# Zero products and a new order in the first pairs' chains, and the first two tiles' activations kept by slots

## The chip, the cores and the metric

The kernel runs on one core of a Trainium2 chip. The core has a matrix engine (TensorE, PE in the profile; PEld is its weight load), three engines that work on elements (VectorE is DVE, ScalarE is ACT, GpSimd is POOL), and a queue engine, SyncE (SP), that here only issues DMA transfers. ACT issues DMA transfers too, between its copies. PE writes to PSUM, eight banks of 2 KB a partition, and DVE or ACT must copy a result out before a bank is used again. The metric is the device time of one execution in microseconds (us). Three timed runs of the kernel before gave 237.89, 238.70 and 238.92 us, a median of 238.7 us.

## The reference

Two layers follow each other. The first is a linear attention with decay (4 batches, 8 heads, 768 positions, head size 64); the second a bilinear feed-forward layer on the 3072 tokens that come out of it.

```python
gamma = 1.0 - 2.0 ** (-5.0 - np.arange(H))
for t in range(S):
    state = gamma[None, :, None, None] * state + np.einsum('bhd,bhe->bhde', k[:, :, t], v[:, :, t])
    y[:, :, t] = scale * np.einsum('bhd,bhde->bhe', q[:, :, t], state)
x = y.transpose(0, 2, 1, 3).reshape(B * S, H * D)        # 3072 x 512
out = (x @ w_a) * (x @ w_b) @ w_out                       # 512 -> 1536 -> 512
```

Inputs and outputs are float32; the kernel multiplies in bfloat16.

## The kernel before

**Attention.** Tokens are cut into 24 slots of 128 positions, six to a batch. Within a slot the recurrence is written as a masked product: scores of k and q, a mask, a product with v (`intra`), and a product of q with the state from earlier slots (`inter`); `update` adds the slot to the state. The decay is put into k and q by tables (`scaled`, L211, k times ktab and q times qtab).

The first six slots, the whole of batch 0, are handled as three pairs (`casts2`, `flip2`, `scores2`, `update2`, `intra2`, `inter2`, `leave2`): one load brings 256 positions with even and odd positions side by side, so that a pair's scores come out by even and odd. `casts2` makes the bfloat16 copies `kqb` (K is index 0, Q is index 1) and `vb`; `flip2` transposes them on PE (L348) and copies the result to `kqT`; `scores2` makes `at` (L361) and masks it on DVE into `aT` (L367); `leave2` copies the result `y` into `xt`, one half on ACT (L177) and one on DVE (L179), and in copying it puts even and odd positions back into natural order.

**Feed-forward.** `TILES = [4, 2, 4, 4, 4, 4, 2]` groups the slots into seven tiles of 512 or 256 tokens. Pairs 0 and 1 are tile 0, pair 2 is tile 1. For a tile and each of 12 blocks `ft` of 128 hidden units, `ffn_a` makes the first product (L429) and ACT copies it to `asb` (L432); `ffn_g` makes the second (L439) and DVE multiplies both into `ht` (L441). `ffn_out` makes 128 tokens of the output (L455), ACT copies them to `osb` (L177) and then issues the store of 256 KB to `out` on its own queue (L461). There are four `osb` buffers.

**Order.** `seq` fixes the program order of every engine as written, so each engine works strictly in that order. Loads are issued on SP in the order of `LOADS`: pairs p0 and p1, weights w0 to w4 (POOL casts them, L179), pair p2, w5, the six parts of `w_out`, then slots s6 to s11. From slot 10 on, SP also transposes `kqb` by DMA (L225), and behind the transpose of slot t it issues the loads of slot t+2 (L91).

The first two pairs and tile 0's first blocks are written out by hand. Pair 2 is worked on after block 9 of tile 0, beside blocks 10 and 11. Then `run` works through lists: tile 1's 12 blocks, the four outputs of tile 0 and the two of tile 1 with the turns of slots 6 to 9 between them, then tile 2. In what follows store 0 to store 5 are these six outputs, in order.

**Waits.** DMA transfers report on eight semaphores. The built program gives each transfer one of the eight, and a transfer that is the next on a semaphore waits, on the engine that issues it, until the earlier transfer on it has landed. Loads on SP and stores on ACT share them. In the built program of before, store 0 waits in this way for the v load of slot 8, store 1 for the v load of slot 9, stores 2, 3 and 4 for an earlier store, and store 5 for the q load of slot 13. PSUM for `a`, `g`, `o`, `tp` and some `at` comes in turn from three banks (`psff`); `y` has two banks and the pairs' first `at` two more.

Of the kernel before, what the change touches and what calls it, by code (L numbers as in the profile page):

```python
# [9 lines left out]
F32 = mybir.dt.float32  # L10
BF16 = mybir.dt.bfloat16
# [13 lines left out]
def kernel(  # L25
# [10 lines left out]
    nc = tc.nc  # L36
    P = 128
    B, H, S, D = q.shape
    NCH = S // P
    HP = H // 2  # L40
    DM = H * D
    DFF = moe_w_a.shape[1]
    KT = DM // P
# [29 lines left out]
    def seq(bi):  # L73
        ins = bi.ins
        prev = last.get(ins.engine)
        if prev is not None:
            tc.add_manual_dep(ins, prev.name, nosync, reason="program order")
        last[ins.engine] = ins
        return bi
# [36 lines left out]
    def issue_loads(n):  # L116
        for _ in range(min(n, len(pending))):
            what = pending.pop(0)
            {"p": load_pair, "s": load_slot, "w": load_w, "o": load_o}[what[0]](int(what[1:]))
# [2 lines left out]
    kqb = {}  # L122
    kqb = {}
    issue_loads(6)
    lgr = const.tile([P, 1, H], F32, name="lgr")
    bq = const.tile([P, 1], F32, name="bq")
    for h in range(H):
# [47 lines left out]
    def cast(engine, dst, src):  # L175
        if engine is nc.scalar:
            seq(nc.scalar.copy(dst, src))  # L177
        else:
            seq(engine.tensor_copy(dst, src))  # L179
# [12 lines left out]
    xt, where = {}, {}  # L192
# [7 lines left out]
    def scaled(eng, t, i):  # L200
        ktab, qtab = tabs[0] if t < 2 * PAIRS else tabs[1]
        dst, src, tab = kqb[t][:, i], raws["kq"[i], t], (ktab, qtab)[i][:, t % NCH]
        if t < 2 * PAIRS:
            dst, src = (x.rearrange("p (hp r) d -> p hp r d", r=2) if x is src else x
                        for x in (dst, src))
            tab = tab.rearrange("p (hp r) o -> p hp r o", r=2).to_broadcast([P, HP, 2, D])
        else:
            dst = dst.rearrange("p hp r d -> p r hp d")
            src = src.rearrange("p (r hp) d -> p r hp d", r=2)
            tab = tab.rearrange("p (r hp) o -> p r hp o", r=2).to_broadcast([P, 2, HP, D])  # L210
        seq(eng.tensor_tensor(dst, src, tab, op=ALU.mult))  # L211
# [121 lines left out]
    def casts2(u, on):  # L333
        for t in (2 * u, 2 * u + 1):
            new_nat(t)
        for (i, par), eng in on.items():
            scaled(eng, 2 * u + par, i)
        for t in (2 * u, 2 * u + 1):
            cast(nc.gpsimd, vb[t], raws["v", t])

    def flip2(u, i, on):
        if i == 0:
            kqT2[u] = tra.tile([P, 2, 2, HP, P], BF16, tag="kqT2", name="kqT2", bufs=2)
        for pars, eng in on:
            tp = psff.tile([P, 2, HP, P], BF16, tag="ff", name="tp")[:, : len(pars)]
            for n, par in enumerate(pars):
                for hp in range(HP):
                    seq(nc.tensor.transpose(tp[:, n, hp, :], kqb[2 * u + par][:, i, hp, :, :], ident))  # L348
            cast(eng, kqT2[u][:, pars[0] : pars[0] + len(pars), i], tp)
# [37 lines left out]
    def inter2(u):  # L387
        for c in range(2):
            if (u, c) == (0, 0):
                continue  # L390
            for hp in range(HP):
                seq(nc.tensor.matmul(ys[u][c][:, hp, :], gbd[c][:, hp, :],
                                     kqT2[u][:, :, 1, hp, half(c)], start=False, stop=False,
                                     skip_group_check=True))

    def intra2(u, par, begin):
        if begin:
            ys[u] = [psat.tile([P, HP, P], F32, tag=f"y{c}", name="y") for c in range(2)]
        t = 2 * u + par
        for hp in range(HP):  # L400
            for r in range(2):
                for c in range(2):
                    seq(nc.tensor.matmul(ys[u][c][half(r), hp, :], vb[t][half(c), 2 * hp + r, :],  # L403
                                         aT[t][half(c), r, hp, :],
                                         start=(begin and hp == 0), stop=not begin,
                                         skip_group_check=True))

    def leave2(u):
        J, i = where[2 * u]
        if i == 0:  # L410
            xt[J] = xtp.tile([P, KT, 4 * P], BF16, tag="xt", name="xt")
        for c, eng in enumerate((nc.scalar, nc.vector)):
            cast(eng,
                 xt[J][:, :, (i + c) * P : (i + c + 1) * P].rearrange(
                     "p k (n two) -> p k two n", two=2),
                 ys[u][c].rearrange("p k (two n) -> p k two n", two=2))

    ht = {}

# [2 lines left out]
    def ffn_a(J, ft, c0=0, c1=None):  # L422
        c1 = TILES[J] * P if c1 is None else c1
        if J not in ht:
            ht[J] = htp.tile([P, NFT, 4 * P], BF16, tag="ht", name="ht")
        fs = slice(ft * P, (ft + 1) * P)
        a = psff.tile([P, 4 * P], F32, tag="ff", name="a")[:, : c1 - c0]
        for kt in range(KT):
            seq(nc.tensor.matmul(a, wa_bf[:, kt, fs], xt[J][:, kt, c0:c1],  # L429
                                 start=(kt == 0), stop=(kt == KT - 1)))  # L430
        asb = asbs[J, ft, c0] = asbp.tile([P, 4 * P], BF16, tag="asb", name="asb")[:, : c1 - c0]
        seq(nc.scalar.copy(asb, a))  # L432

    def ffn_g(J, ft, c0=0, c1=None):
        c1 = TILES[J] * P if c1 is None else c1
        fs = slice(ft * P, (ft + 1) * P)
        g = psff.tile([P, 4 * P], F32, tag="ff", name="g")[:, : c1 - c0]
        for kt in range(KT):
            seq(nc.tensor.matmul(g, wb_bf[:, kt, fs], xt[J][:, kt, c0:c1],  # L439
                                 start=(kt == 0), stop=(kt == KT - 1)))  # L440
        seq(nc.vector.tensor_tensor(ht[J][:, ft, c0:c1], g, asbs.pop((J, ft, c0)), op=ALU.mult))  # L441

# [4 lines left out]
    def ffn_out(J, i):  # L447
        n0 = (sum(TILES[:J]) + i) * P
        osb = osbp.tile([P, DM], F32, tag="osb", name="osb")
        ends = J == len(TILES) - 1 and i == TILES[J] - 1  # L450
        cols = [(0, DM // 2), (DM // 2, 3 * DM // 4), (3 * DM // 4, DM)] if ends else [(0, DM)]
        for c0, c1 in cols:
            o = psff.tile([P, DM], F32, tag="ff", name="o")[:, : c1 - c0]
            for ft in range(NFT):
                seq(nc.tensor.matmul(o, ht[J][:, ft, i * P : (i + 1) * P], wo_bf[:, ft, c0:c1],  # L455
                                     start=(ft == 0), stop=(ft == NFT - 1)))
            cast(nc.vector if c0 == DM // 2 else nc.scalar, osb[:, c0:c1], o)
            if c0 == DM // 2:
                continue
            b0 = DM // 2 if c0 else 0  # L460
            seq((nc.sync if c0 else nc.scalar).dma_start(out=out[n0 : n0 + P, b0:c1],  # L461
                                                         in_=osb[:, b0:c1]))

    def run(work, todo, ahead=4):
        order = []
# [10 lines left out]

    D_, G_, A_ = nc.vector, nc.gpsimd, nc.scalar
    K, Q = 0, 1
    casts2(0, {(K, 1): D_, (K, 0): D_, (Q, 1): D_, (Q, 0): D_})
    flip2(0, K, [((0, 1), A_)])  # L480
    flip2(0, Q, [((1,), D_), ((0,), D_)])
    scores2(0, 1)
    scores2(0, 0, True)
    update2(0, 0)
    casts2(1, {(K, 0): G_, (K, 1): G_, (Q, 0): G_, (Q, 1): D_})
    intra2(0, 1, True)
    inter2(0)
    intra2(0, 0, False)
    leave2(0)
    flip2(1, K, [((0, 1), A_)])  # L490
    update2(0, 1)
    flip2(1, Q, [((1,), D_), ((0,), D_)])
    scores2(1, 0)
    scores2(1, 1, True)
    update2(1, 0)
    cast_w(0)
    W2 = 2 * P
    intra2(1, 0, True)
    inter2(1)
    ffn_a(0, 0, 0, W2)  # L500
    ffn_a(0, 1, 0, W2)
    intra2(1, 1, False)
    leave2(1)
    issue_loads(100)
    cast_w(1)
    ffn_g(0, 0, 0, W2)
# [5 lines left out]
    for ft in range(2, NFT):  # L512
        if ft == 3:
            late_tables()
        if ft % FPW == 0 and ft // FPW + 1 < NW - 1:
            cast_w(ft // FPW + 1)
        if ft == 8:
            casts2(2, {(K, 0): G_, (Q, 0): G_})
            cast_w(NW - 1)
        if ft < 10:  # L520
            ffn_ab(0, ft)
        if ft == 8:
            scaled(D_, 5, K)
            scaled(D_, 5, Q)
    flip2(2, K, [((0, 1), A_)])
    flip2(2, Q, [((0, 1), D_)])
    scores2(2, 0)
    update2(2, 0)
    ffn_a(0, 10)
    scores2(2, 1)  # L530
    ffn_a(0, 11)
    intra2(2, 0, True)
    inter2(2)
    ffn_g(0, 10)
    intra2(2, 1, False)
    leave2(2)
    ffn_g(0, 11)
    for j in range(NO):
        cast_o(j)
# [46 lines left out]
```

## Time and profile before

| | |
|---|---|
| median of three timed runs | 238.7 us (237.89 to 238.92) |
| the profiled execution | 237.4 us, span 235.7 us |
| PE busy | 219.6 us, 93% of the span |
| DVE, ACT, POOL busy | 41%, 35%, 33% |
| DMA moved | 38.59 MB, mean 164 GB/s |
| first product | 6.5 us after the start |
| tile 0's full-width blocks begin | 24.2 us |
| tile 1's first block | 47.0 us |
| tile 2's first block | 78.8 us |

The profile is one execution. A group of instructions has a line, an engine, its tiles, a count and a duration; what stands in brackets is the idle time of the engine before it and what ended that. "ACTq" and "SPq" are transfers being issued on ACT and SP. "DMA share" in the windows is the mean number of packets in flight at one of 16 DMA engines, so it can be over 1. The granted clock of TensorE reads 1.00 in every stretch.

### The profile page before, as it was taken

The numbers are of one execution on the slowest core, as the hardware profiler recorded it, in microseconds if no ns is written. First come the engines' busy times: TensorE is split into PE (matmuls) and PEld (weight loads), VectorE is DVE, ScalarE is ACT, GpSimd is POOL, SyncE is SP. The second block draws the span as 40 slices with busy tenths as digits, with TensorE's granted clock in tenths as the row PEclk, the third lists the DMA queues.
The fourth block names the chain that finished last, engine by engine and source line by source line (L and its number), as shares of the span: only waits on it lengthen the run. The fifth ranks groups of instructions, "written<-read, shape, count | busy, mean of one in ns | idle before, by whom it ended". The sixth has DMA issues, their size and how long they took to land.

```text
span 235.7 us, 4955 instructions
## 1 busy us (share of the span) xinstructions
PE 219.6 (93%) x2021; PEld 121.6 (52%) x2044; DVE 96.1 (41%) x170; ACT 83.2 (35%) x162; POOL 78.6 (33%) x99
## 2 busy tenths in 40 slices
PE   0788997999999899999999999999999999999995
PEld 0566444488555344545454544454544444445874
DVE  3766347655254055634045640155630124310530
ACT  2243523443114423524234521344512242312422
POOL 3385766787763454445335530000000000000000
PEclk9999999999999999999999999999999999999999
DMA  6999999999999999999999982200002200012102
GB/s 179 290 333 352 335 273 376 342 198 219 234 260 211 245 252 172 243 181 257 210 255 172 230 93 89 89 4 0 3 0 89 89 3 0 0 47 89 45 3 89
DMA packets 91894, 38.59 MB, mean 164 GB/s; under 512 B 71776, under 2 KB 87392, under 8 KB 91872
## 3 DMA queue, kind: packets, MB, share of 16 engines
q1 hardware_dynamic: 88416, 32.12, 64.4%
q10 hardware_dynamic: 3456, 6.16, 7.3%
q8 instruction: 16, 0.26, 0.5%
q14 instruction: 6, 0.05, 0.1%
HBM read 28.31 MB, written 6.29 MB: 147 GB/s over the span
## 4 chain that ended last, share of the span: by engine, by line
PE 77%; DMA 11%; DVE 5%; issue 2%; SPq 2%; POOL 1%; ACT 1%; ACTq 0%; DVEq 0%; POOLq 0%
PE g L439 24%; PE a L429 24%; PE o L455 20%; DMA kf<-in_k_dram 6%; DMA qf<-in_q_dram 5%; PE at L254 2%; PE y L299 1%; DVE aT L367 1%; POOL kqb L211 1%; SPq L91 1%; PE tp L348 1%; PE st L270 1%; PE y L403 1%; DVE ht L441 1%; DVE kqT L179 1%
## 5 line engine op out<-in xcount | busy, mean ns | idle before, releaser
L441 DVE TENSOR_TENSOR ht<-g,asb 128x512 bf16<-128x512 f32 (+1 forms) x86 | 52.0, 604 | 109.8 <-PE g L439 88.7
L439 PE MATMUL g<-xt,wb_bf 128*128 128x512 bf16 (+1 forms) x340 | 76.0, 344 | 1.7 <-ACT asb L432 0.8
L429 PE MATMUL a<-xt,wa_bf 128*128 128x512 bf16 (+1 forms) x334 | 75.3, 344 | 0.8 <-DVE xt L179 0.2
L432 ACT CAST asb<-a 128x512 bf16<-128x512 f32 (+1 forms) x86 | 44.2, 517 | 69.4 <-PE a L429 63.6
L455 PE MATMUL o<-wo_bf,ht 128*128 128x512 bf16 (+2 forms) x303 | 63.7, 362 | 0.5
L439 PEld LDWEIGHTS <-wb_bf 128*128 128x128 bf16 x344 | 33.4, 98 | 30.3 <-issue 1.3
L429 PEld LDWEIGHTS <-wa_bf 128*128 128x128 bf16 x344 | 32.7, 98 | 27.9 <-DVE xt L179 0.7
L455 PEld LDWEIGHTS <-ht 128*128 128x128 bf16 x312 | 29.2, 98 | 31.5
L177 ACT COPY osb<-o 128x512 f32<-128x512 f32 (+2 forms) x25 | 14.1, 565 | 53.2 <-PE o L455 41.2
L211 POOL TENSOR_TENSOR kqb<-kf,ktab 128x512 bf16<-128x512 f32 x21 | 21.9, 1044 | 26.6 <-DMA kf<-in_k_dram 26.6
L211 POOL TENSOR_TENSOR kqb<-qf,qtab 128x512 bf16<-128x512 f32 x20 | 21.4, 1068 | 3.1 <-DMA qf<-in_q_dram 2.4
L259 DVE TENSOR_TENSOR aT<-at,mask 128x512 bf16<-128x512 f32 x36 | 22.3, 680 | 0.0
L179 POOL CAST vb<-vf 128x512 bf16<-128x512 f32 x24 | 14.5, 612 | 20.6 <-DMA vf<-in_v_dram 10.6
L348 PE MATMUL tp<-ident,kqb 128*128 128x128 bf16 x48 | 5.5, 280 | 7.2 <-DVE kqb L211 7.2
L308 ACT CAST xt<-y 128x512 bf16<-128x512 f32 x18 | 9.7, 589 | 3.2 <-PE y L299 3.2
L367 DVE TENSOR_TENSOR aT<-at,mask 128x512 bf16<-128x512 f32 x12 | 7.5, 684 | 2.4 <-PE at L361 2.4
L348 PEld LDWEIGHTS <-kqb 128*128 128x128 bf16 x48 | 4.0, 125 | 8.3 <-DVE kqb L211 7.8
L179 POOL CAST wa_bf<-wsta 128x1024 bf16<-128x1024 f32 x6 | 6.3, 1044 | 4.0 <-DMA wsta<-in_moe_w_a_dram 4.0
L179 POOL CAST wb_bf<-wstb 128x1024 bf16<-128x1024 f32 x6 | 6.3, 1043 | 2.7 <-DMA wstb<-in_moe_w_b_dram 2.7
L179 POOL CAST wo_bf<-wsto 128x1024 bf16<-128x1024 f32 x6 | 6.3, 1042 | 1.9 <-DMA wsto<-in_moe_w_out_dram 1.9
L177 ACT CAST gst<-st 128x256 bf16<-128x256 f32 x12 | 4.5, 373 | 6.7 <-PE st L270 6.7
L254 PE MATMUL at<-kqT 64*64 64x128 bf16 x288 | 5.8, 219 | 0.0
(47 smaller groups left out, 81.9 us busy)
## 6 DMA issues: line engine op xcount, KB each, us to landing
out_dram<-osb ACTq DMA_DIRECT2D x23, 256.0 KB, 2.1
kf<-in_k_dram SPq DMA_DIRECT2D x18, 256.0 KB, 4.6
qf<-in_q_dram SPq DMA_DIRECT2D x18, 256.0 KB, 5.1
vf<-in_v_dram SPq DMA_DIRECT2D x18, 256.0 KB, 5.4
wsta<-in_moe_w_a_dram SPq DMA_DIRECT2D x6, 512.0 KB, 8.8
wstb<-in_moe_w_b_dram SPq DMA_DIRECT2D x6, 512.0 KB, 9.0
wsto<-in_moe_w_out_dram SPq DMA_DIRECT2D x6, 512.0 KB, 8.9
kf<-in_k_dram SPq DMA_DIRECT2D x3, 512.0 KB, 7.1
```

What stands on the lines that cost most here:

```text
L177: seq(nc.scalar.copy(dst, src))
L179: seq(engine.tensor_copy(dst, src))
L211: seq(eng.tensor_tensor(dst, src, tab, op=ALU.mult))
L254: seq(nc.tensor.matmul(at[r][half(c), hp, :], kqT[t][half(r), 0, hp, half(c)], kqT[t][half(r), 1, hp, :], start=True, stop=True, skip_grou ...
L259: seq(nc.vector.tensor_tensor(aT[t][:, r], at[r], mask.to_broadcast([P, HP, P]), op=ALU.mult))
L348: seq(nc.tensor.transpose(tp[:, n, hp, :], kqb[2 * u + par][:, i, hp, :, :], ident))
L367: seq(nc.vector.tensor_tensor(aT[t][:, r], at[r], masks[par].to_broadcast([P, HP, P]), op=ALU.mult))
L429: seq(nc.tensor.matmul(a, wa_bf[:, kt, fs], xt[J][:, kt, c0:c1], start=(kt == 0), stop=(kt == KT - 1)))
L432: seq(nc.scalar.copy(asb, a))
L439: seq(nc.tensor.matmul(g, wb_bf[:, kt, fs], xt[J][:, kt, c0:c1], start=(kt == 0), stop=(kt == KT - 1)))
L441: seq(nc.vector.tensor_tensor(ht[J][:, ft, c0:c1], g, asbs.pop((J, ft, c0)), op=ALU.mult))
L455: seq(nc.tensor.matmul(o, ht[J][:, ft, i * P : (i + 1) * P], wo_bf[:, ft, c0:c1], start=(ft == 0), stop=(ft == NFT - 1)))
```

## The change

1. A tile `zero` (128 x 4 x 128, bfloat16) is set to zero on DVE ahead of the other tables. `warm(n, ...)` issues n products of 128x512 of `zero` with itself into a PSUM bank that nothing reads. There are 11 before the first transposes, then 3, 1, 3, 4, 4 and 2 between the steps of pairs 0 and 1; the first 22 use the bank `y1`, the last six a bank of `psff`.
2. Pair 1's Q for even positions is scaled on DVE and not on POOL. Pair 1's K is transposed before the second `intra2` of pair 0. Of pair 1's two score steps the other one uses the `psff` banks. Tile 0's first two half-width `ffn_a` stand before pair 1's `intra2` and `inter2`.
3. `xt` of tiles 0 and 1 is kept as [P, 4 slots, KT, P], and `leave2` copies `y` as it lies, with even positions first, without reordering; pair 0's two copies are both on ACT. `xcols` gives the products their columns from it.
4. Since the columns of tiles 0 and 1 are then in even-odd order, the store of their outputs puts the rows back: the destination is `(n two) d -> two n d`. In the built program stores 0 to 5 are transfers to a pattern of 2 x 64 x 512, where before they were 128 x 512. The other 19 stores are as before.
5. Pair 2: both K are scaled on POOL (issued ahead of block 7) and both Q on DVE, and its chain starts after block 7 of tile 0 and is spread over blocks 8 to 11.

In the built program the semaphores of the transfers fall differently: store 0 now waits for the k load of slot 9, store 1 for the q load of slot 10, store 3 for the k load of slot 12, store 5 for the v load of slot 13; store 2 waits for store 0, store 4 for store 2, and the copy into store 5's `osb` for store 1.

```diff
+    zero = const.tile([P, HP, P], BF16, name="zero")
+    seq(nc.vector.memset(zero, 0.0))
...
-    def leave2(u):
+    def leave2(u, on):
         J, i = where[2 * u]
         if i == 0:
-            xt[J] = xtp.tile([P, KT, 4 * P], BF16, tag="xt", name="xt")
-        for c, eng in enumerate((nc.scalar, nc.vector)):
-            cast(eng,
-                 xt[J][:, :, (i + c) * P : (i + c + 1) * P].rearrange(
-                     "p k (n two) -> p k two n", two=2),
-                 ys[u][c].rearrange("p k (two n) -> p k two n", two=2))
+            xt[J] = xtp.tile([P, 4, KT, P], BF16, tag="xt", name="xt")
+        for c, eng in enumerate(on):
+            cast(eng, xt[J][:, i + c], ys[u][c])
+
+    def xcols(J, kt, c0, c1):
+        if J < 2:
+            return xt[J][:, c0 // P : c1 // P, kt, :]
+        return xt[J][:, kt, c0:c1]
+
+    def warm(n, pool, tag):
+        idle = pool.tile([P, HP, P], F32, tag=tag, name="idle")
+        for _ in range(n):
+            seq(nc.tensor.matmul(idle, zero[:, 0, :], zero, start=True, stop=True,
+                                 skip_group_check=True))
...
-            seq((nc.sync if c0 else nc.scalar).dma_start(out=out[n0 : n0 + P, b0:c1],
-                                                         in_=osb[:, b0:c1]))
+            dst, src = out[n0 : n0 + P, b0:c1], osb[:, b0:c1]
+            if J < 2:
+                dst = dst.rearrange("(n two) d -> two n d", two=2)
+            seq((nc.sync if c0 else nc.scalar).dma_start(out=dst, in_=src))
...
+    warm(11, psat, "y1")
     casts2(0, {(K, 1): D_, (K, 0): D_, (Q, 1): D_, (Q, 0): D_})
     flip2(0, K, [((0, 1), A_)])
-    flip2(0, Q, [((1,), D_), ((0,), D_)])
+    warm(3, psat, "y1")
+    flip2(0, Q, [((1,), D_)])
+    warm(1, psat, "y1")
+    flip2(0, Q, [((0,), D_)])
+    warm(3, psat, "y1")
     scores2(0, 1)
     scores2(0, 0, True)
     update2(0, 0)
-    casts2(1, {(K, 0): G_, (K, 1): G_, (Q, 0): G_, (Q, 1): D_})
+    warm(4, psat, "y1")
+    casts2(1, {(K, 0): G_, (K, 1): G_, (Q, 1): D_, (Q, 0): D_})
     intra2(0, 1, True)
     inter2(0)
+    warm(4, psff, "ff")
+    flip2(1, K, [((0, 1), A_)])
     intra2(0, 0, False)
-    leave2(0)
-    flip2(1, K, [((0, 1), A_)])
+    leave2(0, (A_, A_))
     update2(0, 1)
     flip2(1, Q, [((1,), D_), ((0,), D_)])
-    scores2(1, 0)
-    scores2(1, 1, True)
+    warm(2, psff, "ff")
+    scores2(1, 0, True)
+    scores2(1, 1)
     update2(1, 0)
     cast_w(0)
     W2 = 2 * P
+    ffn_a(0, 0, 0, W2)
+    ffn_a(0, 1, 0, W2)
     intra2(1, 0, True)
     inter2(1)
-    ffn_a(0, 0, 0, W2)
-    ffn_a(0, 1, 0, W2)
     intra2(1, 1, False)
-    leave2(1)
+    leave2(1, (A_, D_))
...
-        if ft == 8:
-            casts2(2, {(K, 0): G_, (Q, 0): G_})
+        if ft == 7:
+            casts2(2, {(K, 0): G_, (K, 1): G_})
             cast_w(NW - 1)
-        if ft < 10:
+        if ft < 8:
             ffn_ab(0, ft)
-        if ft == 8:
-            scaled(D_, 5, K)
-            scaled(D_, 5, Q)
+    scaled(D_, 5, Q)
+    scaled(D_, 4, Q)
     flip2(2, K, [((0, 1), A_)])
+    ffn_a(0, 8)
     flip2(2, Q, [((0, 1), D_)])
+    ffn_g(0, 8)
+    ffn_a(0, 9)
     scores2(2, 0)
     update2(2, 0)
-    ffn_a(0, 10)
+    ffn_g(0, 9)
     scores2(2, 1)
-    ffn_a(0, 11)
     intra2(2, 0, True)
     inter2(2)
+    ffn_a(0, 10)
+    intra2(2, 1, False)
+    leave2(2, (A_, D_))
+    ffn_a(0, 11)
     ffn_g(0, 10)
-    intra2(2, 1, False)
-    leave2(2)
     ffn_g(0, 11)
```

More of the change, by code (lines that the diff above doesn't have):

```diff
@@ L428, in ffn_a @@
         for kt in range(KT):
-            seq(nc.tensor.matmul(a, wa_bf[:, kt, fs], xt[J][:, kt, c0:c1],
+            seq(nc.tensor.matmul(a, wa_bf[:, kt, fs], xcols(J, kt, c0, c1),
                                  start=(kt == 0), stop=(kt == KT - 1)))
@@ L438, in ffn_g @@
         for kt in range(KT):
-            seq(nc.tensor.matmul(g, wb_bf[:, kt, fs], xt[J][:, kt, c0:c1],
+            seq(nc.tensor.matmul(g, wb_bf[:, kt, fs], xcols(J, kt, c0, c1),
                                  start=(kt == 0), stop=(kt == KT - 1)))
```

## The prediction

> **What bounds the kernel now.** I read the page first. PE is busy in nearly every slice, so time is lost only where PE stands still, and the DMA row says that up to slice 25 (about 147 us) transfers run without a break.
>
> ```profile
> PE   0788997999999899999999999999999999999995
> DMA  6999999999999999999999982200002200012102
> q10 hardware_dynamic: 3456, 6.16, 7.3%
> out_dram<-osb ACTq DMA_DIRECT2D x23, 256.0 KB, 2.1
> ```
>
> Next the timeline, for the three places where PE stands still before tile 2: the start, pair 2, and 81 us. The same 32 score products took 1.07 us of PE at 9.42 and 0.64 at 16.37, so early products run at little more than half speed. Pair 2's K is ready on POOL only once its load is there, at 32.40.
>
> ```profile
> 6.50 1.04 PE L348 MATMUL tp<-ident,kqb 128*128 128x128 bf16 x8 [6.50 <-DVE kqb L211]
> 9.42 1.07 PE L361 MATMUL at<-kqT 64*64 64x128 bf16 x32 [0.51 <-DVE kqT L179]
> ...
> 16.37 0.64 PE L361 MATMUL at<-kqT 64*64 64x128 bf16 x32 [0.51 <-DVE kqT L179]
> ...
> 32.40 1.04 POOL L211 TENSOR_TENSOR kqb<-kf,ktab 128x512 bf16<-128x512 f32 x1 [0.69 <-DMA kf<-in_k_dram]
> ...
> 47.01 0.61 PE L429 MATMUL a<-xt,wa_bf 128*128 128x256 bf16 x4 [0.18 <-DVE xt L179]
> ```
>
> Then the chain of waits, which from 54 to 82 us runs through loads and POOL, and leaves them at one point:
>
> ```profile
> 74.98 6.14 DMA qf<-in_q_dram
> ...
> 81.19 0.34 ACTq L461
> 81.53 0.04 issue
> 81.57 0.59 ACT asb L432
> 82.17 0.04 issue
> 82.21 1.02 PE g L439 x4
> ```
>
> ACT cannot issue store 5 until slot 13's q load has landed (81.12), since both report on one semaphore; `asb` is queued behind it on ACT, and PE needs the bank that `asb` frees. So at 82.21 a load, not PE, sets the time: PE restarts 1.09 us after the landing. Whatever the first 80 us gain is lost there unless that landing moves. The windows, with DMA share second to last, show that the DMA engines have no room around it, and the DMA view gives the issues of that stretch and the next load's landing, slot 13's v: issued at 77.03, so landed at about 82.2.
>
> ```profile
> 60.00:65.00 5.00, 5.00 (x76) 2.84 (x75) 1.60 (x3) 1.24 (x3) 3.86 (x5) 1.00 1.29 240
> 70.00:80.00 10.00, 9.89 (x137) 5.26 (x138) 2.81 (x5) 4.24 (x8) 3.83 (x5) 1.00 1.22 236
> ```
> ```profile
> 77.03 0.80 SPq L91 DMA_DIRECT2D vf<-in_v_dram  x1
> ```
> ```profile
> vf<-in_v_dram SPq DMA_DIRECT2D x1, 256.0 KB, 5.2
> ```
> ```profile
> out_dram<-osb ACTq DMA_DIRECT2D x6, 256.0 KB, 4.2
> ```
>
> After 82 us PE has hardly a gap, so what moves that restart moves the end one for one.
>
> **Part 1: zero products and pairs 0 and 1.** Clearing `zero` costs about 0.28 us on DVE (two of that size, the `gbd` clears, took 0.55); what it pushes back, the decay's exponents (1.25 to 1.46, so at worst to 1.74), is awaited by ACT, whose table load lasts until 2.08, so it is hidden. The first 11 products take 11 x 0.216 us (a steady 128x512 product) to twice that, 2.4 to 4.8, from about 1.3 us: over by 6.1, before K is ready at 6.49. Three products after K's transposes (0.65 to 1.3) meet a gap of only 0.2 us, so Q's transposes can slip by 0.3 to 1.0; the rest stand where PE waits for copies. Against this, if PE is at full speed from the first chain on, its rows shrink as the 32 scores did, 0.4 us each for scores, and less for states and `y`: about 1.5 together, part of it beside DVE's masks (2.48 us a pair). Q of pair 1 on DVE saves POOL 1.54 us, and the second Q is ready at about 13.9 in place of 14.2. The last `g` no longer waits for DVE's `xt` (0.65). Moving two `ffn_a` ahead fills PE's wait for pair 1's masks. The next thing late is w1's second half, cast on POOL at 21.51 to 22.55 behind its load: block 2 can start at about 21.7 in place of 24.2, not earlier. I take 2.5 gained by block 2; ends 0 and 3.
>
> The Trainium skill ("TensorE: Matmul & The Clock Gate", Part 1) says that PE runs at half rate until about 3.4 us of sustained activity. The granted clock reads 1.00 throughout and does not show it, the durations do; by that rule the 11 products would put the whole chain at full rate.
>
> **Part 2: pair 2.** Its K is gated by the load: POOL ends at 33.44 and, for the second K, 34.5. With 2.5 gained, PE has done six blocks (two of 0.86 each make 1.73) at 21.7 + 10.4 = 32.1 and waits. From 34.5 on PE has 16 transposes (0.9), scores (0.9), states (0.4), `y` (1.0) and four blocks (6.9), 10.1 us, plus about 0.4 of waits: tile 1 starts at 45.0, in place of 47.0. In the old order the same work took 12.6 (34.4 to 47.0). Both Q on DVE (0.68 each, or 1.52 beside POOL, as at 37.78) are covered by block 8's first product. SP issues the same transfers in the same order, and POOL has the same count of casts. Gain 2.0; ends 0 and 3.
>
> **Part 3: `xt` by slots.** Copies that are contiguous cost at most what the strided ones did (0.74); pair 0's two on ACT last 1.5 instead of 0.74, and nothing reads them for 3 us. Products read the same number of columns. I cost it at nothing; if the strided reads slowed products, tile 0's blocks would show it.
>
> **Part 4: the stores.** Two things change. First the semaphores: store 3 now waits for slot 12's k load (landed 72.97), store 5 for slot 13's v load, 82.2 instead of 81.12. Queued behind store 3 on ACT are a state copy, slot 6 and 7's `xt` copies and the next `osb`; PE needs those `y` banks, so it loses about 1.5 of the 2.0 already there. At store 5 it loses the rest and more: restart at 82.2 + 1.09 = 83.3 against 82.21, so +1.1 if nothing else happens to the loads.
>
> Second, the pattern. Every transfer of before starts with 128 parts on both sides; stores 0 to 5 now start with 2 parts on the DRAM side. No row shows what that does to the spread over the 16 DMA engines, so I bound it. Below: nothing, +1.1. Above: one engine carries a store. The store queue's 3456 packets took 7.3% of 16 x 235.7, 275 us: 80 ns a packet, 11.7 us for each of 23.5 stores, 0.73 on each of 16 engines. On one engine that is 11 us extra a store. On two, 5.9 on each, 5.1 extra. A load lands when its slowest engine is done, and the share of 1.22 to 1.29 says no engine is free; packets overlap by that factor, so a store delays the loads by 5.1 / 1.25 = 4.1 us (one engine: 8.8). Stores 0 to 3 are ahead of slot 13's v load: 4 x 4.1 = 16.4 (one engine: 35). I take two engines, since the pattern offers two outer parts. Then the v load lands at 98.6, PE restarts at 99.7: +17.5 against 82.21.
>
> The skill's page "DMA: Bandwidth & Descriptors", section "Rules for kernel authors", speaks against the change: a transfer uses at most as many engines as its outermost dimension has parts, so two here, and it should have 128 outermost; by that rule +17.5 stands, and without it +1.1.
>
> Waits of store 2 for store 0 and 4 for 2 lie in the same stretch: on two engines a store alone needs 5.9 us, beside loads perhaps 8 to 12, so they hold ACT at times, but end before 98.
>
> **Sum.** Gains of parts 1 and 2 (2.0) are spent before the restart, so they do not count. 237.4 + 17.5 = 254.9; the profiled execution is 1.3 under the median, so 256 for a timed run, 255.5 rounded down because slot 13's load may pass part of store 3.
>
> **Rivals.**
> - A, the stores stay spread: 238.7 + 1.1 = 239.8. For it: 2 KB packets as before, and no row of a short first dimension. Against: the built pattern.
> - B, faster: stores spread, and slot 13's v load lands early. The one mechanism is that store 5 is no longer in flight beside it. The time is under 237.5, faster by over 0.5%, if that load lands before 79.9, 2.3 earlier than it did; before 79.1 all of the 2.0 survive: 236.7. Against: with a share of 1.22 the loads have no idle engine to gain from.
> - C, slower than the sum: the waits of store 2 for 0 and 4 for 2 come one after another. A store waits 2.1 us more beside loads than alone (4.2 against 2.1) with 8 packets an engine; with 64 that may be 8 x 2.1 more, an estimate of about 23 a store with its own 5.9, and two such waits hold ACT until 59.4 + 46 = 105 or later: 262 and up.
>
> **How the numbers follow.** The forecast (two engines, 246 to 262) gets 0.69, C 0.13, A 0.12, B 0.06. The range 243 to 266 leaves out A, B and the upper part of C, about 2 in 10. A measurement tells 0.5%, 1.2 us, from no change. A lies near that bound and is split, 0.07 same and 0.05 slower; B is faster, the rest slower. That the zero products do nothing, or pair 2's order gains nothing, changes none of it but B: PE only has to reach store 5 before its load lands.
>
> **What would show it.** Right: stores 0 to 5 taking 6 us and more to land against 4.2, loads in that stretch landing several us later than 5, PE still at 85 to 98 us behind `asb` behind a store, and block 2 at about 21.7, tile 1 at 45. Wrong: the stores land in 3 to 5 us. Then A or B holds, and the time is that of slot 13's v load.

## The result, and the profile after

The changed kernel takes 261.08 us (median of four runs, 260.02 to 261.86) against 238.81 us before (four runs). The ratio is 1.094, with a 95% interval from 1.088 to 1.101: 22.3 us slower. The forecast was 255.5 us in a range from 243 to 266, for the reason that was then found; but one term of its sum was too small, one standstill came at another place, and the slow products after a standstill were not in it.

The page of the profiled execution (260.65 us, span 258.9 us) shows the loss at once. One character is 6.5 us:

```profile
PE   6989889999940490999999999999999999999995
PEclk9999999999995577799999999999999999999999
DMA  7999999999338938999999999221000210003102
q10 hardware_dynamic: 3372, 6.16, 6.7%
```

PE is busier at the start than before (slice 0 has 6, where it had 0), and then has a hole in slices 11 to 15, from 71 to 104 us, with a full slice of work only in slice 14. In slices 10, 11 and 14 the DMA row falls to 3, although loads are outstanding. The packets of the queue that carries the stores are a little fewer than before (3372, 3456), so the stores were not cut into smaller pieces. PE's clock, full in every slice before, falls to 0.5 in the hole.

The timeline of PE, wherever it stood still between 60 and 105 us (the columns are start, busy time, operation, count, and the idle time with its releaser):

```profile
87.17 0.26 PE L292 MATMUL y<-kqT,gst 64*64 64x128 bf16 x1 [12.79 <-ACT xt L310]
...
103.74 1.87 PE L449 MATMUL g<-xt,wb_bf 128*128 128x512 bf16 x4 [7.00 <-ACT asb L442]
```

There are two standstills, 12.79 and 7.00 us, both behind ACT. ACT's own lines name what it waited for: first slot 12's k load, for the semaphore of store 3, then slot 13's v load, for that of store 5:

```profile
85.65 0.52 ACTq L474 DMA_DIRECT2D out_dram<-osb  x1
86.27 0.37 ACT L179 CAST gst<-st 128x256 bf16<-128x256 f32 x1 [15.50 <-DMA kf<-in_k_dram]
...
102.54 0.52 ACTq L474 DMA_DIRECT2D out_dram<-osb  x1
103.11 1.07 ACT L442 CAST asb<-a 128x512 bf16<-128x512 f32 x2 [8.33 <-DMA vf<-in_v_dram]
```

The chain of waits, which before ran through q of slot 13 to 82.21, ends at the same place, later, behind v of slot 13:

```profile
87.92 14.54 DMA vf<-in_v_dram
...
102.54 0.52 ACTq L474
103.06 0.04 issue
103.11 0.59 ACT asb L442
103.70 0.04 issue
103.74 1.87 PE g L449 x4
```

That load was issued at 87.92 in place of 77.03, because SP's queue was itself held up, and took 14.54 us in place of 5.2. PE went on at 103.74 in place of 82.21: 21.5 us. The remaining 1.7 of the 23.2 by which the span grew are the first eight products after the standstill, at half rate (the chain gives 1.87 and 1.71 us for four each, where before it gave 1.02 and 0.86).

The DMA view, narrowed to 74 to 86 us (one character is now 0.3 us), shows why the loads were late:

```profile
DMA  9991111111111111179911111111894699999999
GB/s 265 294 230 59 47 46 46 53 53 46 46 47 54 53 46 46 47 177 245 131 46 47 53 44 32 36 37 36 165 276 112 138 267 249 255 271 257 220 216 230
```

A 1 is a tenth of the 16 engines, and two of 16 are 0.125. For 4 us on end only about two engines work, at about 50 GB/s together; the others have finished their part, and no new load reaches them, since SP itself stands at one transfer from 73.15 to 81.64 (its line is shown at the end).

The completions that the trace records count the engines. A 256 KB load is reported by 16 completions, and so is a plain store; I read them as one for each engine. In the kernel before, the 16 of slot 13's v load come within 0.1 us, at 82.15 to 82.23. In the changed kernel 14 of them come at 96.5 to 96.8 and the last two at 102.43 and 102.47. A store in two parts is reported by two: those of stores 0 to 4 come at 69.5, 75.6, 81.6, 95.1 and 101.1 us, 9 to 13 us after their issue, and about 6.0 us apart where one store follows another. So five stores pass through the two engines ahead of the load that holds store 5, and its last two parts land behind them.

The head did what it was to do, in part. The first products are the zero products, then K's transposes, then pair 0's scores; the last lines are a new wait at 28 us, and tile 1's first blocks:

```profile
1.25 4.33 PE L425 MATMUL idle<-zero 128*128 128x512 bf16 x11 [1.25 <-DVE zero L126]
6.38 0.62 PE L350 MATMUL tp<-ident,kqb 128*128 128x128 bf16 x8 [0.80 <-DVE kqb L213]
...
9.16 0.64 PE L363 MATMUL at<-kqT 64*64 64x128 bf16 x32
...
22.65 1.04 PE L439 MATMUL a<-xt,wa_bf 128*128 128x512 bf16 x4
...
28.18 1.02 PE L449 MATMUL g<-xt,wb_bf 128*128 128x512 bf16 x4 [1.04 <-ACT asb L442]
...
45.88 0.60 PE L439 MATMUL a<-xt,wa_bf 128*128 128x256 bf16 x4
```

The eight transposes take 0.62 us in place of 1.04, the 32 scores 0.64 in place of 1.07, and block 2 starts at 22.65 in place of 24.20. Tile 1 starts at 45.9 in place of 47.0. So 1.55 us were gained at block 2, and 1.1 us are left at tile 1.

### The profile page after: what moved, and what is told of

It is laid out like the page before. It is cut to its first block, busy times and chain, and to the rows that moved or that the text cites. A ratio compares the mean times of both kernels' runs of the same rounds, so it can differ in the third digit from the quotient of the medians.

```text
span 258.9 us, 5015 instructions
## 1 busy us (share of the span) xinstructions
PE 228.9 (88%) x2051; PEld 123.2 (48%) x2072; DVE 96.5 (37%) x171; ACT 82.6 (32%) x163; POOL 77.5 (30%) x98
## 3 DMA queue, kind: packets, MB, share of 16 engines
q10 hardware_dynamic: 3372, 6.16, 6.7%
## 4 chain that ended last, share of the span: by engine, by line
PE 65%; DMA 17%; SPq 10%; POOL 2%; DVE 2%; issue 1%; ACT 1%; ACTq 0%; DVEq 0%; POOLq 0%
PE g L449 21%; PE a L439 21%; PE o L465 18%; DMA kf<-in_k_dram 8%; DMA vf<-in_v_dram 6%; DMA wstb<-in_moe_w_b_dram 4%; SPq L97 3%; SPq L227 3%; SPq L105 2%; SPq L91 2%; PE at L256 2%; PE y L301 1%; POOL kqb L213 1%; PE st L272 1%; DVE kqb L213 1%
## 5 line engine op out<-in xcount | busy, mean ns | idle before, releaser
L439 PE MATMUL a<-xt,wa_bf 128*128 128x512 bf16 (+1 forms) x337 | 76.7, 347 | 0.6 <-POOL wa_bf L181 0.2
L465 PE MATMUL o<-wo_bf,ht 128*128 128x512 bf16 (+2 forms) x303 | 65.7, 370 | 0.6 <-issue 0.2
L213 POOL TENSOR_TENSOR kqb<-kf,ktab 128x512 bf16<-128x512 f32 x22 | 22.8, 1042 | 34.9 <-DMA kf<-in_k_dram 33.6
L261 DVE TENSOR_TENSOR aT<-at,mask 128x512 bf16<-128x512 f32 x36 | 22.3, 682 | 0.0
L213 POOL TENSOR_TENSOR kqb<-qf,qtab 128x512 bf16<-128x512 f32 x18 | 18.8, 1042 | 8.5 <-DMA qf<-in_q_dram 8.0
L292 PE MATMUL y<-kqT,gst 64*64 64x128 bf16 x120 | 3.7, 229 | 13.0 <-ACT xt L310 13.0
L425 PE MATMUL idle<-zero 128*128 128x512 bf16 x26 | 8.7, 462 | 1.3 <-DVE zero L126 1.3
L292 PEld LDWEIGHTS <-gst 64*64 64x64 bf16 x120 | 2.5, 112 | 14.0 <-issue 14.0
```

Source lines behind the costliest of these rows:

```text
L261: seq(nc.vector.tensor_tensor(aT[t][:, r], at[r], mask.to_broadcast([P, HP, P]), op=ALU.mult))
L425: seq(nc.tensor.matmul(idle, zero[:, 0, :], zero, start=True, stop=True, skip_group_check=True))
L439: seq(nc.tensor.matmul(a, wa_bf[:, kt, fs], xcols(J, kt, c0, c1), start=(kt == 0), stop=(kt == KT - 1)))
```

## The experiments

The theory: a store whose outer dimension has two parts is carried by two DMA engines; the loads that share those engines, and the semaphores that the stores share with loads, then hold ACT, and ACT holds PE. The rivals: that the shifted semaphores alone do it; that a store with a row stride is slow in any case; that the head or the zero products cost something.

| kernel | median us | ratio to before (95% interval) |
|---|---|---|
| changed kernel | 261.08 | 1.094 (1.088 to 1.101) |
| changed, plain stores | 237.73 | 0.996 (0.993 to 0.999) |
| before, stores in 2 parts | 258.88 | 1.084 (1.082 to 1.085) |
| before, stores in 4 parts | 251.28 | 1.052 (1.048 to 1.056) |
| before, stores in 8 parts | 240.44 | 1.005 (1.002 to 1.009) |
| before, one store in 2 parts | 241.52 | 1.011 (1.006 to 1.016) |
| changed, stores split in halves of 64 rows | 240.91 | 1.006 (1.002 to 1.010) |
| changed, tile 0's stores in 2 parts but late | 236.72 | 0.989 (0.983 to 0.995) |
| changed, token-order xt, plain stores | 237.87 | 0.995 (0.991 to 1.000) |
| the same, store 5 four blocks later | 235.51 | 0.987 (0.982 to 0.991) |
| the same, late tables in two steps | 234.96 | 0.985 (0.981 to 0.989) |
| store 5 later, without zero products | 236.68 | 0.992 (0.989 to 0.995) |
| before, store 5 five blocks later | 238.82 | 0.997 (0.993 to 1.002) |

### The pattern of the stores, undone and done alone

The first kernel leaves out two lines of `ffn_out`:

```diff
             dst, src = out[n0 : n0 + P, b0:c1], osb[:, b0:c1]
-            if J < 2:
-                dst = dst.rearrange("(n two) d -> two n d", two=2)
```

> The changed kernel with the stores of tiles 0 and 1 written as one 128-part by 512 pattern again, as in the kernel before. The rows of these 768 tokens then stay in even-odd order in the output; nothing else differs, and the DMA semaphores that stores 3 and 5 share with loads are those of the changed kernel. Theory (the two-part pattern confines each store to two DMA engines): nearly all of the 22 us go; 239.8 us, between 238 and 241, with PE going on at 83.3 behind store 5. Rival (the shared semaphores and the waits of ACT on loads are the cause, whatever the pattern): 258 to 261. Rival (the head's new order or the zero products throttle the clock): 258 to 261, with the granted clock near 0.95.

Measured: 237.73 us. Of 22.3 us nothing is left, with the shifted semaphores still in place. The rival that blames them, and the one that blames the head, are out. In this kernel's timeline store 5 still waits for slot 13's v load, and PE for `asb` behind it:

```profile
81.00 0.34 ACTq L472 DMA_DIRECT2D out_dram<-osb  x1
81.38 1.07 ACT L442 CAST asb<-a 128x512 bf16<-128x512 f32 x2 [2.69 <-DMA vf<-in_v_dram]
```
```profile
82.02 1.02 PE L449 MATMUL g<-xt,wb_bf 128*128 128x512 bf16 x4 [1.36 <-ACT asb L442]
```

PE goes on at 82.02, against 82.21 before: of the 1.1 us that tile 1 had gained, 0.2 are left behind this wait (called the gate in what follows).

The second kernel adds the pattern, and nothing else, to the kernel before:

```diff
+            if J < 2:
+                dst = dst.rearrange("(n e) d -> e n d", e=2)
```

> The kernel before with one change: the stores of tiles 0 and 1 have two parts of 64 rows as their outer dimension in DRAM (their rows come out in another order than the reference's). Head, order and semaphores are those of before. Theory (two engines a store): four stores lie ahead of the load that gates store 5; the changed kernel showed about 20 us for that, so 259 us, between 254 and 262, and PE standing still at 75 to 100. Rival (semaphores or head): 238.8, between 238 and 240. Rival (ACT needs 0.8 us longer to issue such a store): 240 to 242.

Measured: 258.88 us, 20.0 over the 238.90 of the same comparison. The pattern alone makes 20.0 of the 22.3 us; where the other 2.3 come from is not shown. The chain of waits of this kernel runs through two q loads, each 2.5 to 3.2 times as long as the 5.3 us of a q load in that stretch of the kernel before:

```profile
67.15 16.86 DMA qf<-in_q_dram
...
87.33 13.32 DMA qf<-in_q_dram
...
100.73 0.52 ACTq L464
```

### Four parts and eight

The same edit with `e=4` and `e=8`.

> The kernel before with four parts of 32 rows as the outer dimension of the stores of tiles 0 and 1 (rows in another order). Theory (as many DMA engines as outer parts): a store needs 2.9 us on each of four engines in place of 5.9 on each of two, 2.2 us over the 0.73 of an even spread against 5.1, so 0.43 of the loss with two parts: about 9 us, 247 us, between 244 and 250. Rival (any strided store costs the same, by its issue or its row stride): the same time as with two parts.

> The kernel before with eight parts of 16 rows as the outer dimension of the stores of tiles 0 and 1 (rows in another order). Theory (as many DMA engines as outer parts): 1.47 us on each of eight engines, 0.73 over an even spread, 0.14 of the loss with two parts: about 3 us, 241.5 us, between 239.5 and 243. Rival (any strided store costs the same): the same time as with two parts.

Measured: 251.28 us (12.4 over before) and 240.44 us (1.5 over before). The stride of the rows is not the cause: the strides grow with the number of parts, and the loss shrinks. That the number of parts decides is borne out, its law only roughly. Four parts were to cost about 9 us and cost 12.4, outside the range given; eight were to cost about 3 and cost 1.5, inside it. The DMA view of the four-part kernel, from 81 to 90 us (0.225 us a character), has 2s where two parts have 1s, at about 100 GB/s:

```profile
DMA  2412799999999999999999999999722223248999
GB/s 98 73 65 75 105 116 106 125 112 97 122 101 113 115 101 117 93 101 197 287 167 218 257 248 240 245 238 247 156 80 101 108 81 116 102 147 245 271 322 298
```

A 2 is up to 0.3 of 16 engines, and four of 16 are 0.25. The completions agree: of slot 12's v load, 12 come at 76.6 to 77.3 us and four at 78.6 to 82.4; in the eight-part kernel eight come at 74.1 to 74.5 and eight at 76.9 to 77.0.

The Trainium skill ("DMA: Bandwidth & Descriptors", section "Rules for kernel authors") says that a transfer uses at most as many engines as its outermost dimension has parts. The two rows agree with it: about 50 GB/s and 0.1 of the engines with two parts, about 100 GB/s and 0.2 with four.

### One store of six

Here only store 0 has two parts (`if (J, i) == (0, 0)` in place of `if J < 2`), in the kernel before.

> The kernel before with the first store alone, of six, in two parts (128 rows come out in another order). Theory (each store delays the loads by the same 4 to 5 us, and they add up): 243 us, between 242 and 244.5, PE waiting for q of slot 13 about 4 us longer. Rival (the loss comes from stores that wait for one another on a shared semaphore, with ACT held between them, and one alone has nobody to hold but store 2): 238.8 to 240.5.

Measured: 241.52 us, 2.6 over before (238.91). It falls between the two: less than the 4 to 5 us that the theory gave a store, more than the rival allowed. So one such store delays the loads even when no other follows it. The profiled execution shows the delay itself, and why the time shows less of it:

```profile
70.24 5.16 SPq L91 DMA_DIRECT2D vf<-in_v_dram  x1
...
79.64 5.61 DMA qf<-in_q_dram
...
86.34 1.02 PE L439 MATMUL g<-xt,wb_bf 128*128 128x512 bf16 x4 [1.30 <-ACT asb L432]
```

SP needs 5.16 us to issue slot 12's v load (1.12 before), and slot 13's q load lands at 85.25, 4.1 us later than the 81.12 in the profile of before. But PE waits only 1.30 us there, since in this execution it comes to the gate 3.45 us later than in the profile of before; it is already that much later at tile 1, ahead of the store (the last section returns to this). So 2.6 us, a difference of medians, is not what a store costs a load.

With all six stores in two parts, the kernel before has slot 13's q load landing at 100.65 (the second q load of the chain above), 19.5 us later than in its own profile, with five such stores issued ahead of it (64.87 to 87.10): 3.9 us for each. In the changed kernel it is 20.3 us for five, 4.1 for each. So the delays add up, at about 4 us a store, and a price that rises with their number is not shown. These are single executions: in the kernel before with plain stores and store 5 issued later, the same load landed at 79.46, 1.7 us ahead of the profile of before. No kernel with two or three such stores was run.

### The same pattern where no load runs

The stores of tile 0 keep two parts, but are kept in buffers of their own and issued in tile 5; tile 1's stores are plain:

```diff
+            if J == 0:
+                held.append((dst.rearrange("(n two) d -> two n d", two=2), src))
+                continue
...
-            5: [(4, turn, None, 22)],
+            5: [(4, turn, None, 22)] + [(ft, flush) for ft in (5, 7, 9, 11)],
```

> The changed kernel with the four stores of tile 0 still in two parts, but issued in tile 5, when no load is left; tile 1's two stores are plain (their 256 rows stay in even-odd order). Theory (a store on two engines costs only what it holds up, the loads and the engines that wait for them): 236.5 us, between 235 and 238, the gate at store 5 gone as well. Rival (the pattern is slow in itself, by its issue on ACT or a stall of ACT's queue, wherever it stands): at least 4 us over that, 241 or more.

Measured: 236.72 us. That is 1.2 us over the 235.51 us of a later run that has neither two-part stores nor the gate (it also keeps `xt` in token order and issues store 5 later); so four stores in two parts, with no load beside them, cost about a microsecond. PE's timeline shows 0.49 us of it as one wait, at 216 us, for an `osb` behind the late stores. Their issue on ACT is slower there too, 1.09 and 0.52 us against 0.34, and that holds nobody. The DMA view from 185 to 215 us (0.75 us a character) shows the four stores issued at 191.6 to 202.0 as a long row of 1s:

```profile
DMA  0000000000011111111111112111111372183164
GB/s 3 0 0 0 0 0 0 0 0 0 16 33 30 33 44 49 52 52 49 52 52 49 55 49 74 52 49 52 52 49 52 139 246 74 60 287 115 49 251 158
```

With no load on the chip the pattern still gets 49 to 52 GB/s: it is a limit of the transfer, not of contention. 262 KB at 50 GB/s are 5.2 us a store, and the last completions of the four stores come 5.1 us apart (199.5, 204.6, 209.8 and 214.9 us). The prediction had 5.9. The plain stores at the right end reach about 250 GB/s.

### Halves of 64 rows

Each store is cut in two transfers, `dst[two]` from `osb[64 * two : 64 * two + 64]`, so the rows come out in token order and the outer dimension has 64 parts.

> The changed kernel with each two-part store cut in two transfers of 64 rows, so that the outer dimension has 64 parts and the result is in token order; 12 stores in place of 6, so the semaphores that they share with loads move again, and the last half of store 5 shares one with slot 14's k load. Theory (the outer dimension decides): 239 us, between 237.5 and 241, the later gate included. Rival (the row stride of two in DRAM is what costs): 258 or more.

Measured: 240.91 us, inside the range, near its upper end. Nearly all of the pattern's cost is gone, with the rows still two apart in DRAM: 3.2 us are left over plain stores (237.73). PE's timeline has two waits behind ACT that plain stores do not have, 1.92 us at 73.7 and 1.91 at 78.3. So the row stride of two is not what costs. Twice as many transfers meet twice as many shared semaphores, and ACT stands between the halves of a store. Its lines for the stores (x2 counts the halves, and the time includes the wait between them):

```profile
68.09 4.90 ACTq L475 DMA_DIRECT2D out_dram<-osb  x2
73.03 0.58 ACT L179 COPY osb<-o 128x512 f32<-128x512 f32 x1 [4.97 <-DMA kqT<-kqb]
73.64 3.67 ACTq L475 DMA_DIRECT2D out_dram<-osb  x2
77.42 0.37 ACT L179 CAST gst<-st 128x256 bf16<-128x256 f32 x1 [3.80 <-DMA vf<-in_v_dram]
```

### The head alone, and the gate behind it

Next the changed kernel with `xt` in token order again (the old copies, the old slices) and plain stores: the zero products and the new orders, and nothing of parts 3 and 4.

> The changed kernel with xt in token order and plain 128-row stores: the zero products and the new orders of pairs 0 to 2 alone, with store 5 still ahead of tile 2's copies on ACT. Theory (the slot layout of xt costs and gains nothing by itself): the time of the changed kernel with plain stores, 237.7 us, between 237.0 and 238.4. Rival (contiguous xt copies or reads gain something that the stores hid): 238.5 or more.

Measured: 237.87 us, against 237.73 with `xt` by slots. The layout of `xt` costs nothing and brings nothing by itself; its only effect on the time was that it asked for the two-part stores.

To this kernel one thing is done: store 5 is put on a list and issued after four blocks of tile 2, by when the semaphore that it shares has been released long ago.

```diff
+            if (J, i) == (1, 1):
+                held.append((dst, src))
+                continue
...
-    todo = {2: [(4, turn, 10, None),
+    todo = {2: [(4, flush), (4, turn, 10, None),
```

> The changed kernel with xt in token order and plain 128-row stores, as in the kernel before (so it has the zero products and the new orders of pairs 0 to 2 alone), and with store 5 issued on ACT after four blocks of tile 2 rather than ahead of them; by then the semaphore that it shares has long been released. Theory (the head and pair 2 gain 1.0 us at tile 1, and ACT's wait at store 5 for a load of slot 13 eats it): with the plain stores PE waits 1.36 us at 82.0; without the wait that much is kept, 236.4 us against 238.8 before, between 235.5 and 237.2. Rival (another load takes over as the gate within the next 20 us): 237.7, as with the wait.

Measured: 235.51 us, 2.4 less than with store 5 in its old place, and 1.3% less than before. Between 44 and 210 us PE's timeline now shows no wait for another engine. What the head gains is real, and it was the wait at store 5 that ate it. The time is 0.9 us under the theory's 236.4, at the lower end of its range; the 1.36 us of waiting that the theory went by explain only part of the 2.4. The same edit in the kernel before:

> The kernel before with one change: store 5 is issued on ACT after five blocks of tile 2. Theory (the wait at 82.2 costs PE 0.62 us in the kernel before): 238.2 us, between 237.5 and 238.6. Rival (a later gate takes over): 238.8.

Measured: 238.82 us, ratio 0.997 (0.993 to 1.002). This one settles nothing: the 0.6 us at stake are smaller than the scatter of the kernel before.

Then the zero products are taken out of the version with the later store 5 (all `warm` lines):

> The same as the kernel with token-order xt, plain stores and store 5 issued four blocks later, without the 28 zero products. Theory (the zero products put the first chain at full rate, 1.55 us at block 2, of which about 1.0 reaches tile 1): the transposes of pair 0 take 1.04 us again and its scores 1.07, and the time is 0.5 to 1.2 us longer than with them: 237.3. Rival (the gain at block 2 is due to the order alone, or is absorbed behind pair 2's load): the same time, 236.4.

Measured: 236.68 us, 1.17 more than with them, as the theory had it (0.5 to 1.2). Without them the first rows are slow again:

```profile
9.44 1.07 PE L363 MATMUL at<-kqT 64*64 64x128 bf16 x32 [0.52 <-DVE kqT L181]
...
16.05 1.07 PE L363 MATMUL at<-kqT 64*64 64x128 bf16 x32 [0.52 <-DVE kqT L181]
...
17.47 1.89 PE L440 MATMUL a<-xt,wa_bf 128*128 128x256 bf16 x8
```

With them the scores take 0.64 both times, the eight `a` products 1.05, block 2 starts at 23.43 in place of 24.90, and tile 1 at 45.9 in place of 47.0. One reservation: without the zero products the stores also came to share their semaphores with other transfers, though PE's timeline shows no wait that this caused.

Last, the wait at 28 us that is new in the changed kernel. There ACT stood 2.9 us before the late decay tables, with two `asb` copies behind them, since VectorE's part waited for GpSimd, and GpSimd for a weight load. The edit leaves GpSimd's part at block 3 and moves the other two engines' part to block 6:

```diff
             if ft == 3:
-                late_tables()
+                posp1 = late_tables()
+            if ft == 6:
+                tables(posp1, 1)
```

> The same as the kernel with store 5 issued four blocks later, and besides, the late decay tables are made in two steps: GpSimd's part at block 3 as before, VectorE's and ScalarE's three blocks later, so that ScalarE does not wait 2.9 us for them at 27.2 with an asb behind. Theory (that wait costs PE 1.0 us at 28.2, and only the Q chain of pair 2 behind it, not the load of its K, sets what follows): tile 1 starts at 45 in place of 46, 235.5 us, between 234.8 and 236.2. Rival (pair 2's K, ready at 34.4 by its load, absorbs it): the same time as without the second edit, 236.4.

Measured: 234.96 us, the fastest of all, 1.5% under the kernel before. Tile 1 starts at 44.80, 1.1 earlier, which is the theory's number:

```profile
34.48 0.40 PE L353 MATMUL tp<-ident,kqb 128*128 128x128 bf16 x4 [0.54 <-POOL kqb L216]
...
35.77 0.62 PE L353 MATMUL tp<-ident,kqb 128*128 128x128 bf16 x8
...
44.80 0.60 PE L443 MATMUL a<-xt,wa_bf 128*128 128x256 bf16 x4
...
74.07 0.41 PE L295 MATMUL y<-kqT,gst 64*64 64x128 bf16 x15 [0.28 <-ACT xt L313]
```

K's wait for its load takes 0.54, but Q's transposes come at 35.77 in place of 36.88. The wait at 28 us is only part of that: in the kernel to which the edit was made it took PE 0.29 us and not 1.0 (its block 2 started 0.8 later than the changed kernel's). Block 2 started 0.25 earlier here, and VectorE's scaling of both Q took 1.28 us in place of 1.69. Of the 1.1 us only some 0.3 are left in tile 2 (the states after its fourth block start at 84.59, against 84.86): PE now waits at 73.6 and 74.1 behind store 3, issued at 72.24 when slot 12's k load has landed. The medians differ by 0.55 us and the runs overlap (234.75 to 235.36, and 234.97 to 235.88), so that this edit makes the kernel faster is likely and not certain.

## Why the prediction was right, and where not

- **What bounds the kernel.** Right. The chain ends at the same place before and after, ACT's store 5 with `asb` behind it, and PE restarts 1.27 us after the load's landing (102.47 to 103.74; 1.09 before). In the new order, moving store 5 alone gave 2.4 us.
- **Two engines a store.** Right: 50 GB/s and 0.1 of the engines, alone as beside loads, two completions a store, and undoing the two lines takes back everything. That was a choice between one engine and two, argued from the pattern, as no row of before showed it. The sign that was named, 6 us and more to land, came: 9 to 13 us.
- **4 x 4.1 = 16.4 us.** The term that was mis-sized. Slot 13's v load landed at 102.47 where 98.6 was forecast; against 82.2 that is 20.3 in place of 16.4. What was too low is the number of stores: five, not four, were issued before that load was through (store 4 at 88.14, the load at 87.92). The 4.1 a store came out (20.3 for five; 4.1 for one alone), but partly by luck: the engine time in it was too high (5.9; alone it measured 5.2), and the delay reached the load in a way that is not in the working. The sum let the load's transfer take longer. In the trace 9.3 us are that (14.54 in place of 5.2), and 10.9 are a later issue, since SP, held at earlier transfers, came to it at 87.92 in place of 77.03.
- **Waits between stores "end before 98".** Right as far as it went, but store 3's wait was costed at 1.5 us of lost head start. Slot 12's k load, which store 3 waits for, landed about 13 us later than before (store 3 was issued at 85.65), and PE's longer standstill, 12.79 us, was there. The restart at store 5 comes after it, so the sum, which went by the last gate alone, was not hurt by this. The 8 to 12 us that a store was to need beside loads were 9 to 13.
- **The semaphores alone: +1.1.** Too high: with plain stores PE restarted at 82.02, 0.2 before the old time, not 1.1 after it. Slot 13's v load landed at about 81.0 in that execution, not at 82.2. Rival A's 239.8 was measured as 237.7, between A's time and B's.
- **Part 1.** Hidden zero products: right (the first 11 end 0.8 us before K is ready). The feared slip of Q's transposes did not come: they start at 7.58 in place of 7.70, since the transposes ahead of them had become shorter. The gain at block 2 was 1.55, where 2.5 was taken.
- **Part 2.** Tile 1 started at 45.9, forecast 45.0; the gain was 1.1 and not 2.0. The missing 0.9 goes with the wait of 1.04 at 28 us: the late tables stood ahead of `asb` on ACT, which the working had not looked at, as ACT's wait there (1.43 before) held nobody. With the tables in two steps tile 1 started at 44.8, though part of that gain lay elsewhere, as said above.
- **Part 3** at nothing: right (237.87 and 237.73).
- **After the restart** nothing was to differ. Instead 1.7 us were lost there, since PE came out of the standstill at half rate. This, the 3.9 us of the mis-sized term and 0.2 us at the restart are the distance from the sum's 254.9 to the 260.65 of the profiled execution.

The Trainium skill ("TensorE: Matmul & The Clock Gate", Part 1) gives about 3.4 us of activity until the full rate. The trace agrees roughly: the eleven zero products from 1.25 on took 4.33 us, between the 2.4 of full rate and the 4.8 of half rate, and the transposes at 6.38 are at full rate.

## What to carry to other kernels

Look at the outermost dimension of every transfer's pattern, on both sides: a reordering of rows that is free for the engines that compute can leave 14 of 16 DMA engines idle for the store that undoes it. When transfers and an engine's instructions share a queue, ask what each transfer waits for and who stands behind it; a store whose result no engine needs held PE here, and only when it was issued four blocks later did the new head's gain reach the end. An early gain is kept only as far as the next gate lets it pass, so find that gate before valuing the gain.

## What the runs showed of the hardware that was not expected

- A standstill of PE costs more than its length. In both standstills the granted clock fell to 0.50, two to four us after the last product. After the longer one, with PE at work again from 87.17, it came back to 1.00 only at about 93.6; after the shorter one (7.00 us) products ran at half rate for 3.6 us from the restart at 103.74, and the window from 100 to 110 us has 0.66.
- The kernel before starts in more than one way. In the profile of before the eight `a` products of pair 1 took 1.04 us; in the profile of the kernel with one two-part store, whose instructions are the same up to there, they ran at half rate, and it had a dip of the clock to 0.50 at 44 to 46 us besides:

```profile
19.70 1.92 PE L429 MATMUL a<-xt,wa_bf 128*128 128x256 bf16 x8
```

  Its first store was issued 3.5 us later than in the profile of before, with no edit ahead of it, while the loads of that stretch were not issued later. So medians of this kernel mix starts that differ by more than most effects asked for here.
- The transfer with few engines slows SP's issue of the following loads as well: in the changed kernel the issues of q and v at 62 and 67 us took 4.75 and 5.81 us on SP, where with plain stores they took 1.42 and 0.87. Neither waited for its semaphore (the transfers ahead on it had landed by 57.4 and 59.8 us). Of the 8.49 us of the transposing transfer after them, 4.5 are a wait for POOL, until 77.63, which itself waited for a late k load:

```profile
62.45 4.75 SPq L91 DMA_DIRECT2D qf<-in_q_dram  x1
67.24 5.81 SPq L91 DMA_DIRECT2D vf<-in_v_dram  x1
73.15 8.49 SPq L227 DMA_TRANSPOSE kqT<-kqb  x1
```

  So a slow transfer on one queue reaches another queue twice, by the engines and by the issue.
